# Moving each DMA transpose from behind a stored output to between the loads

## The chip, the cores and the metric

The kernel runs on one core of one Trainium2 chip. The metric is the device time of one execution in microseconds (us), where lower is better. Before the change the median of the first three executions was 312.18 us (311.15 to 312.39). Each comparison below names the number of executions. Now and then an execution is slower than the rest of the same kernel at a lower TensorE clock; the record calls one slow that is over 1.5% above the fastest.

## The reference

The reference is a retention layer (attention with a decay in place of softmax) followed by a two-layer block with the activation h·cos(h):

```python
# q, k, v: (8 batches, 8 heads, 576 positions, 64) float32
scores = (1 / sqrt(64)) * q @ k.transpose(0, 1, 3, 2)
ret    = scores * Dmat          # gamma[h] ** (i - j) for i >= j, else 0
attn   = ret @ v                # -> x: 4608 tokens x 512
h      = x @ w_in               # w_in: 512 x 2048
out    = (h * cos(h)) @ w_out   # w_out: 2048 x 512; out: 4608 x 512 float32
```

## The kernel before

The 4608 tokens are 36 groups of 128. Each group goes through these steps:

1. `load`: three DMAs (q, k, v; 256 KB each) bring the group in. SyncE (SP) issues them.
2. `prep`: GpSimd scales q and k by the decay and casts them to bf16 (tile `qks`), and casts v.
3. `transposes`: the matmuls of the scores read q and k with the head dimension on the partitions (tile `qkT`, 64 x 128 in the timelines below). For groups 0 to 7 TensorE does it; from group 8 on it is one DMA transpose from `qks` to `qkT`, which SP issues too.
4. `scores`, `state`, `attn_out`, `mm1`, `mm2`: the matmuls on TensorE. The order of TensorE's instructions is fixed by hand.
5. The output of the group is copied out of PSUM by ScalarE and stored by a DMA that SP issues as well.

So one queue, that of SP, issues loads, transposes and stores, one after the other in the order of the program (its timelines below show S7, T16, L19, S8, T17 before, and S7, L19, T17, S8 after). What is issued when is decided in `feed(s)`, which runs right behind the store of group `s`:

```python
def transposes(g, banks=None, only=(0, 1)):
    qks, vb, qkT, qT = tiles["a", g]
    if g >= N_PE_T:                                   # N_PE_T = 8
        nc.sync.dma_start(qkT, qks.rearrange("s m h d -> s (m h d)"), transpose=True)
        return
    ...  # cut: the same on TensorE, for groups below 8

def mm2(n, tsi, et, c0=0, c1=DM):
    ...  # cut: one output matmul; at the last one of a group:
        nc.scalar.copy(ot, ps)
        s = starts[n] // P + tsi
        nc.sync.dma_start(out[s * P : (s + 1) * P, c0:c1], ot)   # the store of group s
        feed(s)

def feed(s):
    nonlocal loaded, prepared, transposed
    while transposed < min(prepared, s + 10):
        transposes(transposed)
        transposed += 1
    while loaded < min(NG, 2 * s + 8, s + 13):
        load(loaded)
        loaded += 1
    while prepared < min(NG, loaded, 2 * s + 7, s + 11):
        prep(prepared)
        prepared += 1
        if transposed < N_PE_T:
            transposed += 1
```

The scores of two groups are issued together. The pair that matters here is 16 and 17, near the end of the stage of groups 8 to 11:

```python
def scores2(g):
    if g < NG:
        scores(g, "a")
        scores(g + 1, "b")
...  # cut
(52, lambda: (attn_out([g + 2, g + 3], "m"), scores2(g + 4))),   # g = 12 here
```

In this text S8 is the store of group 8, L19 the three loads of group 19, T17 the DMA transpose of group 17.

## Time and profile before

| | before |
|---|---|
| span of the profiled execution | 309.7 us |
| TensorE (PE) busy | 299.9 us, 97% |
| PE's longest wait after the start | 1.3 us, on the transpose T17 |
| T17 issued / landed | 113.53 / 118.17 us |
| groups whose scores follow their transpose's landing by under 1 us | 11, 15, 17 |

In the profiles, PE is TensorE, PEld its weight loads, DVE VectorE, ACT ScalarE, POOL GpSimd, SP SyncE; a q behind a name (SPq) means that engine's instruction queue, and PEclk is the clock that TensorE was granted. L173 is line 173 of the kernel; L173 makes the scores (`sc`), L287 the output matmuls (`o`). PSUM is where this kernel has the results of its matmuls.

From the page of the kernel before: the line of PE, the slices of the PE clock and of the DMA engines (each digit is a tenth, 40 slices), and the chain of work that ended last, by engine.

```profile
span 309.7 us, 5653 instructions
...
PE 299.9 (97%) x2328; PEld 171.5 (55%) x2361; DVE 176.1 (57%) x179; ACT 116.8 (38%) x136; POOL 97.4 (31%) x120
...
PEclk9999999999999999999999999999999999999999
DMA  8999999999999999999991899379935510110012
...
PE 89%; SPq 5%; DMA 4%; issue 1%; ACT 0%; DVE 0%; ACTq 0%
```

TensorE bounds the kernel (97% busy, 89% of the chain), so a change to DMA order can only be worth what PE waits for DMA. The second thing to see is the DMA row: for the first 20 slices, some 155 us, the DMA engines are at 8 or 9 tenths. In that stretch a transfer lands when its turn in the queue has come (e6 and e7 below test this: each load added ahead of L19 put its landing off by about 1.4 us).

From the wait view for PE, before: who PE waited for, in us in total, how often, and the longest.

```profile
engine line waited for: us in total, times, longest us
PE o L287 <- issue: 1.6, 10, 0.2
PE sc L173 <- DMA qkT<-qks: 1.3, 1, 1.3
```

The ten pieces of "issue" are missing records and not waits: 33 matmul records are absent here (2328, against 2361 in the profile after), and the line is gone in a profile that has them all. The 1.3 us is the one wait that the order of the transposes can reach. In the timeline of PE, before, it stands at 118 us (start, time taken, what, and in brackets the idle time before it):

```profile
116.51 0.40 PE L173 MATMUL sc<-qkT 64*128 64x128 bf16 x8
118.21 0.40 PE L173 MATMUL sc<-qkT 64*128 64x128 bf16 x8 [1.31 <-DMA qkT<-qks]
118.77 2.54 PE L287 MATMUL o<-w_out_sb,gT 128*128 128x512 bf16 x11 [0.16 <-issue]
```

The scores of group 16 run at 116.51, those of group 17 have to wait. In the row of the weight loads the gap before group 17 is 1.48 us:

```profile
118.21 0.23 PEld L173 LDWEIGHTS <-qkT 64*128 64x128 bf16 x8 [1.48 <-DMA qkT<-qks]
```

That measure is used from here on, because with it the accounts further below come out to 0.02 us.

Why T17 is late shows in the timeline of SP, before, around its issue:

```profile
107.34 1.17 SPq L298 DMA_DIRECT2D out_dram<-ot  x1
108.62 1.30 SPq L146 DMA_TRANSPOSE qkT<-qks  x1
109.97 0.70 SPq L107 DMA_DIRECT2D fq<-in_q_dram  x1
110.72 0.63 SPq L107 DMA_DIRECT2D fk<-in_k_dram  x1
111.39 0.97 SPq L107 DMA_DIRECT2D fv<-in_v_dram  x1
112.46 0.96 SPq L298 DMA_DIRECT2D out_dram<-ot  x1
113.53 1.33 SPq L146 DMA_TRANSPOSE qkT<-qks  x1
```

These are S7, T16, L19 (three rows), S8, T17. SP is never idle between them, and it is far behind: S7 is issued at 107.34 us, while ScalarE copied that output at 85.29 us. T17 comes behind S8 although its data were ready by 105 us.

### The profile page before, as it was taken

Reading aid. Unit: us, or ns where it says so; the run is one execution under the profiler, and the core shown is the slowest. Engines: PE = TensorE matmul, PEld = TensorE weight load, DVE = VectorE, ACT = ScalarE, POOL = GpSimd, SP = SyncE. Lnnn points to the kernel's source line nnn. Section 1 sums busy time; section 2 is a strip of 40 time slices with the busy share of each in tenths; the row PEclk is TensorE's granted clock in tenths of the full one; section 3 lists DMA queues with packets and bytes.
Section 4 is the critical chain, followed back from the end, with each engine's and each line's share of the span. In section 5 each row is a group of like instructions: output and inputs, shape, how many; then the busy total and the mean of one; then the engine's idle time right before and its main releaser. Section 6 shows DMA issues by size and latency. Waiting matters only on the chain.

```text
span 309.7 us, 5653 instructions
## 1 busy us (share of the span) xinstructions
PE 299.9 (97%) x2328; PEld 171.5 (55%) x2361; DVE 176.1 (57%) x179; ACT 116.8 (38%) x136; POOL 97.4 (31%) x120
## 2 busy tenths in 40 slices
PE   8899999999999998999999999999999999999996
PEld 3578547757588554445544554455445544554444
DVE  5766425555777764665567655755576556724610
ACT  2666234715045211650264116511551056015611
POOL 2740066644553564361533153305430000000000
PEclk9999999999999999999999999999999999999999
DMA  8999999999999999999991899379935510110012
GB/s 209 213 210 207 202 231 218 204 217 213 196 231 193 225 235 202 235 208 162 232 248 40 189 214 236 43 153 238 228 62 70 135 37 0 36 68 34 2 64 71
DMA packets 148697, 49.65 MB, mean 160 GB/s; under 512 B 138688, under 2 KB 144192, under 8 KB 148672
## 3 DMA queue, kind: packets, MB, share of 16 engines
q1 hardware_dynamic: 144448, 45.10, 75.3%
q0 software_dynamic: 4224, 4.19, 8.2%
q8 instruction: 18, 0.29, 0.4%
q14 instruction: 7, 0.06, 0.1%
HBM read 36.70 MB, written 9.44 MB: 149 GB/s over the span
## 4 chain that ended last, share of the span: by engine, by line
PE 89%; SPq 5%; DMA 4%; issue 1%; ACT 0%; DVE 0%; ACTq 0%
PE h L270 40%; PE o L287 38%; SPq L107 3%; PE ov L243 3%; PE sc L173 3%; DMA fv<-in_v_dram 2%; PE st L201 2%; PE ov L230 2%; DMA qkT<-qks 1%; PE tr L151 1%; SPq L146 0%; DVE xT L255 0%; SPq L298 0%; SPq L325 0%; ACT vb L158 0%
## 5 line engine op out<-in xcount | busy, mean ns | idle before, releaser
L287 PE MATMUL o<-w_out_sb,gT 128*128 128x512 bf16 (+2 forms) x583 | 131.1, 368 | 2.6 <-issue 1.6
L270 PE MATMUL h<-xT,w_in_sb 128*128 128x512 bf16 (+2 forms) x826 | 127.1, 313 | 0.5
L279 DVE TENSOR_TENSOR gT<-h,cosh 128x1024 bf16<-128x1024 f32 x72 | 88.2, 1225 | 57.5 <-ACT cosh L278 57.4
L270 PEld LDWEIGHTS <-w_in_sb 128*128 128x128 bf16 x832 | 75.9, 98 | 50.2 <-issue 0.4
L278 ACT ACTIVATE cosh<-h,half_pi 128x1024 f32<-128x1024 f32 x72 | 80.2, 1114 | 51.8 <-PE h L270 51.8
L287 PEld LDWEIGHTS <-gT 128*128 128x128 bf16 x608 | 55.2, 98 | 56.9 <-issue 0.6
L132 POOL TENSOR_TENSOR qks<-fq,gq 128x512 bf16<-128x512 f32 x32 | 33.4, 1043 | 109.7 <-DMA fq<-in_q_dram 109.7
L296 ACT COPY ot<-o 128x512 f32<-128x512 f32 (+2 forms) x38 | 21.4, 564 | 121.8 <-PE o L287 117.0
L133 POOL TENSOR_TENSOR qks<-fk,gk 128x512 bf16<-128x512 f32 x35 | 36.5, 1043 | 11.6 <-DMA fk<-in_k_dram 10.0
L182 DVE TENSOR_TENSOR ret<-sc,tri 128x1024 bf16<-128x1024 f32 x32 | 37.9, 1216 | 2.9 <-PE sc L173 2.9
L210 DVE TENSOR_TENSOR sb<-st,diag_105 128x512 bf16<-128x512 f32 x32 | 22.0, 686 | 27.8 <-PE st L201 27.8
L255 DVE CAST xT<-ov 128x1024 bf16<-128x1024 f32 (+1 forms) x17 | 19.7, 1161 | 25.8 <-PE ov L243 25.8
L139 POOL CAST vb<-fv 128x512 bf16<-128x512 f32 x32 | 19.6, 611 | 8.6 <-DMA fv<-in_v_dram 7.1
L201 PEld LDWEIGHTS <-qks 128*128 128x128 bf16 (+1 forms) x128 | 9.2, 97 | 7.5 <-issue 1.3
L201 PE MATMUL st<-vb,qks 128*128 128x128 bf16 (+1 forms) x128 | 12.4, 219 | 0.0
L173 PEld LDWEIGHTS <-qkT 64*128 64x128 bf16 x288 | 8.1, 94 | 7.3 <-ACT qkT L156 2.3
L243 PE MATMUL ov<-ret,vb 128*64 128x128 bf16 x288 | 12.1, 222 | 0.0
L173 PE MATMUL sc<-qkT 64*128 64x128 bf16 x256 | 10.4, 218 | 1.3 <-DMA qkT<-qks 1.3
L230 PEld LDWEIGHTS <-sb 128*128 128x128 bf16 x128 | 8.3, 98 | 4.3 <-issue 0.5
L243 PEld LDWEIGHTS <-vb 128*64 128x64 bf16 x288 | 8.6, 109 | 2.0
L156 ACT COPY qkT<-tr 128x512 bf16<-128x512 bf16 x12 | 6.6, 588 | 8.2 <-PE tr L151 8.2
L230 PE MATMUL ov<-qkT,sb 128*128 128x128 bf16 (+1 forms) x116 | 8.8, 215 | 0.0
(45 smaller groups left out, 54.3 us busy)
## 6 DMA issues: line engine op xcount, KB each, us to landing
out_dram<-ot SPq DMA_DIRECT2D x35, 256.0 KB, 4.1
fk<-in_k_dram SPq DMA_DIRECT2D x32, 256.0 KB, 4.9
fv<-in_v_dram SPq DMA_DIRECT2D x32, 256.0 KB, 5.1
fq<-in_q_dram SPq DMA_DIRECT2D x28, 256.0 KB, 4.3
w_in_sb<-in_moe_w_in_dram POOLq DMA_DIRECT2D x4, 512.0 KB, 8.9
w_out_sb<-in_moe_w_out_dram POOLq DMA_DIRECT2D x4, 512.0 KB, 16.1
fq_110<-in_q_dram SPq DMA_DIRECT2D x2, 512.0 KB, 4.4
fq<-in_q_dram SPq DMA_DIRECT2D x8, 128.0 KB, 4.2
```

The source lines that it names most:

```text
L132: nc.gpsimd.tensor_tensor(out=qks[:, 0], in0=fq, in1=tq, op=ALU.mult)
L133: (nc.vector if g == 3 else nc.gpsimd).tensor_tensor(out=qks[:, 1], in0=fk, in1=tk, op=ALU.mult)
L173: nc.tensor.matmul(ps[:, he, hg, :], lhsT=qkT[d0 : d0 + D, HG + hg, :], rhs=qT[d0 : d0 + D, hg, :], start=True, stop=True,)
L182: nc.vector.tensor_tensor(out=ret.rearrange("p a b i -> p (a b) i"), in0=ps.rearrange("p a b i -> p (a b) i"), in1=mask.unsqueeze(1).to_br ...
L201: nc.tensor.matmul(ps[:, hg, :], lhsT=qks[p0:, 1, 2 * hg : 2 * hg + 2, :].rearrange("s h d -> s (h d)"), rhs=vb[p0:, 2 * hg : 2 * hg + 2, ...
L210: nc.vector.tensor_tensor(out=sb, in0=ps, in1=diag2.unsqueeze(1).to_broadcast([P, HG, P]), op=ALU.mult,)
L230: nc.tensor.matmul(ps[:, x, hg, :n], lhsT=sb[:, hg, :], rhs=qT[:, hg, :n], start=(hg == 0), stop=False, skip_group_check=True,)
L243: nc.tensor.matmul(ps[he * D : he * D + D, x, hg, :], lhsT=vb[:, 2 * hg + he, :], rhs=ret[:, he, hg, :], start=(g % PER == 0 and hg == 0), ...
L270: nc.tensor.matmul(ps[:, j, :], lhsT=w_in_sb[:, dg, (et + j) * P : (et + j + 1) * P], rhs=xT[:, dg, c0 : c0 + w], start=(dg == 0), stop=(d ...
L278: nc.scalar.activation(cosh, ps, ACTF.Sin, bias=half_pi, scale=1.0)
L279: nc.vector.tensor_mul(gT[:, et : et + m, c0 : c0 + w], ps, cosh)
L287: nc.tensor.matmul(ps, lhsT=gT[:, et, tsi * P : (tsi + 1) * P], rhs=w_out_sb[:, et, c0:c1], start=(et == 0), stop=(et == ET - 1),)
```

## The change

Its intent: a transpose should not have to wait for the next stored output. It is issued in the same feed as its own group's `prep`, as soon as two more loads stand behind its group's loads, so that GpSimd has time to prepare it (1.04, 1.05 and 0.61 us for the three instructions of a group in the profile before, from 102.66 us on), and it alternates with loads in place of coming in twos.

```diff
     def feed(s):
         nonlocal loaded, prepared, transposed
-        while transposed < min(prepared, s + 10):
-            transposes(transposed)
-            transposed += 1
-        while loaded < min(NG, 2 * s + 8, s + 13):
-            load(loaded)
-            loaded += 1
-        while prepared < min(NG, loaded, 2 * s + 7, s + 11):
-            prep(prepared)
-            prepared += 1
-            if transposed < N_PE_T:
+        while True:
+            while prepared < min(loaded, NG, 2 * s + 7, s + 11):
+                prep(prepared)
+                prepared += 1
+                if transposed < N_PE_T:
+                    transposed += 1
+
+            if N_PE_T <= transposed < min(prepared, s + 11) and (
+                transposed <= loaded - 3 or loaded == NG
+            ):
+                transposes(transposed)
                 transposed += 1
+            elif loaded < min(NG, 2 * s + 8, s + 13):
+                load(loaded)
+                loaded += 1
+            else:
+                break
```

## The prediction

> What bounds the kernel now. TensorE. PE is busy (page) 299.9 of 309.7 us (97%), and has 89% of the chain of work that ended last. PE's idle gaps sum to about 7 us before its last matmul, and the wait view names the causes: 1.3 us at the start, 1.3 us once in the scores (L173) for a DMA transpose into qkT, 1.6 us "issue" in ten pieces. So the only PE idle time that this change can reach is the waits on transposes.
>
> Why that wait exists. In the timeline of SP, from 31 to 135 us the queue issues without a pause, each 256 KB load about 1.1 us after the one before; the DMA row shows 9 tenths. The queue is late: the store of token group 7 is issued at 107.3 us, though its copy ran on ScalarE at 85 us. So DMA throughput times everything here. From issue, landing and use in the trace, by group (landing to use): group 11 lands 84.49, used 84.53; 15: 107.92, used 108.36; 17: issued 113.53, lands 118.17, PE waits from 116.9 to 118.21. All others have 3.9 us or more.
>
> What changes. Nothing is added or removed, only the queue's order. Before: S2 T8 L10 L11, S3 T9 T10 L12 L13, S4 T11 T12 L14 L15, S5 T13 T14 L16 L17, S6 T15 L18, S7 T16 L19, S8 T17 (S store, T transpose, L load). After: S2 L10 T8 L11 T9, S3 L12 T10 L13 T11, S4 L14 T12 L15 T13, S5 L16 T14 L17 T15, S6 L18 T16, S7 L19 T17, S8. So every odd transpose up to 15, and every one from 16 on, comes one store earlier; 10, 12 and 14 come one load later, but they have 10 to 18 us of slack.
>
> Costs. (1) A store's turn in the queue is 1.0 to 1.1 us, so T11, T15, T17 go that much earlier. (2) A transpose holds SP for 1.3 us against 0.57 us for an unhindered load. After each of the pairs T9 T10, T11 T12, T13 T14 the next load lands 2.24, 1.91, 2.15 us after the transpose before it, where 1.2 is usual; after the single T8 it is 1.2. Estimate from these: the pairs drain the DMA queue for 0.7 to 1.0 us each, and alternating saves about 2.5 us of queue time before T17. Then T17 is issued near 110 to 111 us and lands near 115, before 116.9. The preparation on GpSimd is done in time (group 17: by 105 us). [...] in the trace no transpose before 120 us waited for its own group's preparation.
>
> On the critical path: 1.3 us at 118, and 0 to 1 us in executions where T11 or T15 fall late. Predicted 310.6 us, range 309.6 to 312.0; faster by over 2% 0.01, within 2% 0.98, slower 0.01.
>
> Right or wrong would show: the wait "sc L173 <- DMA qkT" gone or under 0.3 us; PE busy time unchanged; T11, T15, T17 landing 1 to 4 us before use; no double gap in landings at 74 to 99 us; store 8 issued no later than before; span near 308.3 us.
>
> Wrong if the DMA queue gains no time (then about 0.3 us of the wait remains), transposes slow the loads between them, or SP stalls on GpSimd.

## More of the kernel before

The weight loads also show a small wait on T11 at 84 us, which the list of PE hides:

```profile
84.10 0.23 PEld L173 LDWEIGHTS <-qkT 64*128 64x128 bf16 x8 [0.42 <-issue]
84.53 0.22 PEld L173 LDWEIGHTS <-qkT 64*128 64x128 bf16 x8 [0.20 <-DMA qkT<-qks]
```

## The result, and the profile after

| | before | after |
|---|---|---|
| median of 6 executions, same rounds | 311.88 us (311.09 to 312.68) | 309.90 us (309.86 to 310.39) |
| ratio of fast runs | | 0.994 (95%: 0.992 to 0.996) |
| span of the profiled execution | 309.7 us | 308.0 us |
| T17 issued / landed | 113.53 / 118.17 us | 111.83 / 116.07 us |
| wait on T11, on T17 (gap before the weight load) | 0.20, 1.48 us | 0, 0 us |

A ratio is the mean time of one kernel's fast runs over that of the other's of the same rounds, so not quite the ratio of the medians that stand beside it. In these rounds the gain is clear of the noise, though under 2%. On two other chips it was not clear: there the ratios are 0.999 (0.996 to 1.002) and 0.998 (0.996 to 1.001), see e8 and e10.

The same lines of the page, after:

```profile
span 308.0 us, 5686 instructions
...
PE 301.3 (98%) x2361; PEld 171.1 (56%) x2361; DVE 176.1 (57%) x179; ACT 116.8 (38%) x136; POOL 97.3 (32%) x120
...
PEclk9999999999999999999999999999999999999999
DMA  8999999999999999999990999299935310010012
...
PE 92%; SPq 3%; DMA 2%; DVE 1%; issue 1%; ACT 0%; ACTq 0%; DVEq 0%
```

PE's busy time seems to grow by 1.4 us, but no record is missing now: a second profile of the kernel before, which has all 2361 (e5), shows 302.0 us. The chain is now PE to 92%, and its share of DMA and SP has fallen: the piece that led from PE to T17 and on into the SP queue is no longer in it. In the wait view for PE, after, no line names `qkT<-qks` as a DMA any more; these are its first lines:

```profile
engine line waited for: us in total, times, longest us
PE idle L164 <- DVE zeros L351: 1.3, 1, 1.3
PE tr L392 <- DVE qs_111 L381: 0.8, 2, 0.4
PE tr L151 <- POOL qks L133: 0.6, 2, 0.4
```

These three belong to the first 20 us. The timeline of PE shows the scores of 16 and 17 in one piece of 16 matmuls, and the weight loads at 84 us the same for 10 and 11:

```profile
116.31 0.62 PE L173 MATMUL sc<-qkT 64*128 64x128 bf16 x16
116.86 2.76 PE L287 MATMUL o<-w_out_sb,gT 128*128 128x512 bf16 x12
```

```profile
84.10 0.45 PEld L173 LDWEIGHTS <-qkT 64*128 64x128 bf16 x16 [0.42 <-issue]
```

The timeline of SP, after: S7, L19, T17, S8. T17 now comes ahead of S8.

```profile
108.76 0.52 SPq L298 DMA_DIRECT2D out_dram<-ot  x1
109.34 0.42 SPq L107 DMA_DIRECT2D fq<-in_q_dram  x1
109.82 0.69 SPq L107 DMA_DIRECT2D fk<-in_k_dram  x1
110.55 1.17 SPq L107 DMA_DIRECT2D fv<-in_v_dram  x1
111.83 2.14 SPq L146 DMA_TRANSPOSE qkT<-qks  x1
114.06 0.53 SPq L298 DMA_DIRECT2D out_dram<-ot  x1
```

The 1.7 us between the two spans are as long as these two waits: 0.20 + 1.48 = 1.68 us. Whether they are the cause is tested in e4 and in the accounts.

### The profile page after: what moved, and what is told of

It reads as the page before. It is cut to its first block, busy times and chain, and to the rows that moved or that the text cites. A ratio compares the mean times of both kernels' runs of the same rounds, so it can differ in the third digit from the quotient of the medians.

```text
span 308.0 us, 5686 instructions
## 1 busy us (share of the span) xinstructions
PE 301.3 (98%) x2361; PEld 171.1 (56%) x2361; DVE 176.1 (57%) x179; ACT 116.8 (38%) x136; POOL 97.3 (32%) x120
## 4 chain that ended last, share of the span: by engine, by line
PE 92%; SPq 3%; DMA 2%; DVE 1%; issue 1%; ACT 0%; ACTq 0%; DVEq 0%
PE h L270 40%; PE o L287 40%; PE ov L243 3%; SPq L107 3%; PE sc L173 3%; DMA fv<-in_v_dram 2%; PE st L201 2%; PE ov L230 2%; PE tr L151 1%; DVE xT L255 0%; DVE ret L182 0%; SPq L331 0%; ACT vb L158 0%; ACT xT L255 0%; ACT ot L296 0%
## 5 line engine op out<-in xcount | busy, mean ns | idle before, releaser
L287 PE MATMUL o<-w_out_sb,gT 128*128 128x512 bf16 (+2 forms) x608 | 134.8, 368 | 0.3 <-DVE ret L182 0.3
```

What stands on the lines that cost most here:

```text
L287: nc.tensor.matmul(ps, lhsT=gT[:, et, tsi * P : (tsi + 1) * P], rhs=w_out_sb[:, et, c0:c1], start=(et == 0), stop=(et == ET - 1),)
```

## The experiments

Two theories of why T17 no longer comes late. Theory A: its place ahead of the store. Theory B: the alternation with loads, which keeps the DMA queue from draining. The prediction had put 1.0 to 1.1 us on A and about 2.5 us on B. All kernels gave the correct result. The first four ran on one chip, the next four on another, the last two on a third; "before" has its own figure for each. The changed kernel was not run on the first of these chips, so e1 to e4 can be compared with before, but only across chips with the whole change.

### e1: ahead of the store, but still in twos

```diff
-        while transposed < min(prepared, s + 10):   # at the head of feed
-            transposes(transposed)
-            transposed += 1
...
+        while N_PE_T <= transposed < min(prepared, s + 11) and (   # at its end
+            transposed <= loaded - 3 or loaded == NG
+        ):
+            transposes(transposed)
+            transposed += 1
```

> The same transposes in each feed as in the changed kernel (T17 ahead of store 8, T11 ahead of store 4, T15 ahead of store 6), but at the end of the feed behind all its loads, the pairs back to back as before. Theory A (the gain is the place ahead of the store): no wait of the scores for a transpose over 0.2 us, 309.9 to 310.4 us, 1.5 to 2.0 us under before. Theory B (the gain is the alternation, which keeps the DMA queue from draining): the pairs drain the queue again, T17 lands about 1 us later than in the changed kernel (117 us), a wait of about 0.5 us remains, 310.5 us or more.

Measured: 310.93 us median of 6 against 312.48 of 11 before, ratio 0.996 (0.993 to 0.999). In the profile T17 landed at 117.47 us, with a wait of 0.91 us; none on T11. Taken alone this speaks for B, but see the table of landings below.

### e2: alternating, but behind the store

```diff
-        while transposed < min(prepared, s + 10): ...
-        while loaded < min(NG, 2 * s + 8, s + 13): ...
+        due, upto = min(prepared, s + 10), min(NG, 2 * s + 8, s + 13)
+        while transposed < due or loaded < upto:
+            if transposed < due:
+                transposes(transposed)
+                transposed += 1
+            if loaded < upto:
+                load(loaded)
+                loaded += 1
```

> The pairs are broken up by loads, but every transpose stays behind the store that it stood behind before (T17 behind store 8). Theory A: most of the wait remains: T17 lands about 117.3 us (118.2 less at most 0.9 of queue time), wait 0.4 to 1.3 us, 310.7 to 311.8 us. Theory B: no wait, T17 lands before 116.5 us, 309.9 to 310.3 us.

Measured: 311.54 us median of 6, ratio 0.997 (0.994 to 0.999). T17 landed at 117.66 us; waits of 0.58 us on T11 and 0.46 us on T17. B's expectation (no wait, landing before 116.5) fails, and landing, wait and time are all as A expected. Taken alone this speaks for A.

### e3: one swap in the old order

```diff
             prep(prepared)
             prepared += 1
             ...
+        if s == 7:                      # T17 ahead of S8, nothing else
+            transposes(transposed)
+            transposed += 1
```

> One swap in the old order: T17 ahead of store 8 and nothing else. Theory A: the large wait at 118 us is gone or under 0.3 us, the 0.2 us of T11 at 84 us may stay: 310.0 to 310.6 us. Theory B (alternation): T17 gains only its store's turn of about 0.9 us and lands at 117.3 us, a wait of 0.4 us or more remains, 310.6 us or more.

Measured: 310.86 us median of 6, ratio 0.995 (0.992 to 0.998). The timeline of SP of this run shows T16, L19, T17, S8:

```profile
109.38 1.30 SPq L146 DMA_TRANSPOSE qkT<-qks  x1
...
112.11 0.91 SPq L107 DMA_DIRECT2D fv<-in_v_dram  x1
113.13 2.27 SPq L146 DMA_TRANSPOSE qkT<-qks  x1
115.50 0.52 SPq L298 DMA_DIRECT2D out_dram<-ot  x1
```

T17 landed at 117.63 us; waits of 0.62 us on T11, which this kernel does not touch, and 0.40 us on T17. Landing (117.3), wait (0.4 us or more) and time (310.6 us or more) are as B expected, the wait only just. So e1 and e3 speak for B and e2 for A: each half of the change alone left 0.4 to 0.9 us of wait. Waits of this size vary as much between executions of one kernel (e5 below), so the three runs do not decide.

### e4: the order of before, and the scores of 17 later

```diff
-(52, lambda: (attn_out([g + 2, g + 3], "m"), scores2(g + 4))),
+(52, lambda: (attn_out([g + 2, g + 3], "m"), scores(g + 4, "a") if n == 3 else scores2(g + 4))),
+(60, lambda: scores(g + 5, "b") if n == 3 else None),
```

> The DMA order is that of before; TensorE does the scores of group 17 eight output matmuls (1.7 us) later. Theory A and B both say that the one wait at 118 us is the whole loss: no wait or under 0.3 us there though T17 lands near 118 us as before, 310.1 to 310.8 us. If the gain of the change came from elsewhere (faster DMA, other waits), the time stays at 311.5 us or more.

Measured: 310.76 us median of 6, ratio 0.994 (0.992 to 0.997): the size of the gain of the change, with the DMA order untouched. T17 landed at 118.49 us, as late as before, and the weight load after it shows only the 0.42 us that stand ahead of other scores that follow output matmuls, too (those of groups 8, 10 and 12):

```profile
119.06 0.23 PEld L173 LDWEIGHTS <-qkT 64*128 64x128 bf16 x8 [0.42 <-issue]
```

So taking away the wait on T17 is worth a gain of that size, whoever takes it away. A wait of 0.57 us on T11 stayed.

### e5 and e8: both kernels again; e6 and e7: more loads ahead of T17

e5 is the kernel before and e8 the changed kernel, without edits. e6 and e7 put one and two more loads, whose data nobody uses, ahead of L19 and T17 in the changed kernel:

```diff
     def feed(s):
         nonlocal loaded, prepared, transposed
+        for x in range(1 if s == 7 else 0):     # e7: range(2 ...)
+            nc.sync.dma_start(fq4[:, :, x, :], k[0, :, :P, :].rearrange("h s d -> s h d"))
```

> The kernel before, unchanged, for a second profile and the size of its scatter. If the waits on T11 and T17 are the whole difference to the changed kernel, its span is 308.05 us plus those two waits, to about 0.2 us, whatever they are in this execution; T17 lands between 117.5 and 119.5 us.

> The changed kernel with one more 256 KB load (never used) behind store 7, ahead of load 19 and T17. If DMA throughput sets when T17 lands, it lands one load's turn (1.1 to 1.2 us) later, 117.2 us, and the slack of 0.47 us becomes a wait of about 0.7 us: span 308.7 us, time 310.6 us. If the queue has room, nothing changes: 309.9 us.

> The same with two more loads: T17 lands at 118.4 us, a wait of about 1.9 us, span 309.9 us, time 311.8 us. If the queue has room: 309.9 us.

> The changed kernel, unchanged, on the same chip as the three others: 309.9 us within 0.3, no wait of the scores on a transpose over 0.2 us, T17 landing at 115.5 to 116.7 us.

On this chip the kernel before has a median of 311.31 us (7 executions).

- e5: the three fast ones of 4 executions took 310.77, 311.02 and 311.51 us; the fourth, 316.75 us, was slow. In the profile T17 landed at 117.33 us, just outside the expected range, with a wait of 0.71 us and none on T11: the same kernel waited 1.68 us in one execution and 0.71 us in another. The span, 308.89 us, is 308.05 + 0.71 us within 0.2, as expected.
- e8: 310.81 us median of 4 (310.29 to 311.88), ratio 0.999 (0.996 to 1.002), so not shown to be faster than before on this chip. No wait on T11 or T17; T17 landed at 116.52 us. The time missed its range: see the accounts below.
- e6: 314.87, 314.72, 311.45 us and one slow execution (316.19); ratio 1.006 (0.999 to 1.012). The one at 311.45 us ran at full clock, the others at a mean clock of 0.995. T17 landed at 119.35 us; waits of 0.65 us on T11, which stands ahead of the added load, and 2.23 us on T17.
- e7: 315.06 us median of 4, ratio 1.014 (1.009 to 1.019). T17 landed at 119.26 us; a wait of 2.42 us.

From S7's landing to L19's it took 3.52 to 3.57 us in the three profiles of the changed kernel, 4.96 us in e6 and 6.27 us in e7. So each added load of 256 KB costs its full turn, about 1.4 us (estimated at 1.1 to 1.2), and the queue has no room. That theory holds. T17 itself landed 2.2 and 0.9 us later than expected, of which 1.8 and 0.6 us are a later landing of S7, ahead of the added loads. And the spans, 313.0 and 312.9 us, are 4.3 and 3.0 us over what was expected. The added wait explains only part of that; the timeline of PE and the clock row of e7 explain most of the rest:

```profile
116.66 0.40 PE L173 MATMUL sc<-qkT 64*128 64x128 bf16 x8
119.31 0.40 PE L173 MATMUL sc<-qkT 64*128 64x128 bf16 x8 [2.25 <-DMA qkT<-qks]
119.64 2.66 PE L287 MATMUL o<-w_out_sb,gT 128*128 128x512 bf16 x8
```

```profile
PEclk9999999999999997999999999999999999999999
```

There is a 7 in the clock row. The clock records give 0.5 for 3.41 us, from 119.82 us on in e6 and from 120.63 us on in e7, 0.42 and 1.32 us after the scores of 17 began. From the scores of 17 to those of 18 it takes 24.08 us in both, and 22.43 us in the profile of the changed kernel: 1.65 us lost beside the wait itself. (Some 0.4 us more stands after the last matmul in both and has no explanation here.) Half the clock for 3.41 us should cost 3.41 × 0.5 = 1.71 us, an estimate from the clock records of these two profiles, and the trace shows 1.65. The half clock came after 2.06 us (e6) and 2.25 us (e7) of idle PE; after the 1.31 us of the kernel before, the clock stayed full. What sets it off was not tested.

### Landings: what the swap gives, and what the alternation gives

The records of every profile allow the two theories to be read apart. In all of these orders the same transfers stand between S2 and L19 (the extra loads of e6 and e7 apart), so the time from S2's landing to L19's tells what the alternation gives. What comes from L19 to T17 tells what the swap gives. In us:

| kernel | order | S2 to L19 | L19 to T17 |
|---|---|---|---|
| before | in twos, behind | 54.26 | 2.05 |
| e5 (before) | in twos, behind | 53.78 | 1.62 |
| e4 (same DMA order) | in twos, behind | 54.83 | 1.66 |
| e2 | alternating, behind | 54.01 | 1.67 |
| e3 | in twos, T17 ahead of S8 | 54.52 | 0.79 |
| e1 | in twos, ahead | 54.16 | 0.84 |
| after | alternating, ahead | 53.22 | 0.84 |
| e8 (after) | alternating, ahead | 53.47 | 0.82 |
| e10 (after, below) | alternating, ahead | 54.53 | 0.82 |

The last column falls into two groups without overlap: 1.75 us on average behind the store (1.62 to 2.05), 0.82 us ahead of it (0.79 to 0.84). So the swap gives 0.93 us on average, and at least 0.78 us between any two of these profiles. In the third column the old order has a mean of 54.29 and the changed kernel 53.74, a difference of 0.55 us, and executions of one and the same order differ by 1.05 and 1.31 us. Taken over all nine profiles, the five in twos have a mean of 54.31 and the four alternating ones 53.81, 0.50 us less. So about half a microsecond is the best guess for the alternation, and with this scatter these runs do not show that it gives anything. The predicted 2.5 us are not there: even the two profiles furthest apart (54.83 and 53.22) differ by 1.61 us. It also tells why e1, e2 and e3 could not decide by their waits: the size of the wait in one execution is set by this scatter as much as by the order.

### Accounts: where the scatter comes from

For every profile that stays at full clock, the span can be put together from three numbers: the shift of the scores of group 8 (77.78 us in the changed kernel; it tells how long the start took), and the two waits. The last column is the span less that of the changed kernel, 308.04 us.

| profile | start | T11 | T17 | sum | span − 308.04 |
|---|---|---|---|---|---|
| before | 0.00 | 0.20 | 1.48 | 1.68 | 1.69 |
| e5 (before) | 0.14 | 0 | 0.71 | 0.85 | 0.85 |
| e1 | 0.07 | 0 | 0.91 | 0.98 | 0.98 |
| e2 | 0.13 | 0.58 | 0.46 | 1.17 | 1.18 |
| e3 | 0.12 | 0.62 | 0.40 | 1.14 | 1.15 |
| e8 (after) | 0.44 | 0 | 0 | 0.44 | 0.44 |
| e10 (after) | 1.58 | 0 | 0 | 1.58 | 1.60 |

(e4 is left out: its sum is 0.59 us and its span 0.82 us longer, a difference of 0.23 us; the author puts it down to the split pair of scores, which was not tested.) In these profiles there are two sources of scatter, and the change touches one of them. In e10 the start alone took 1.58 us longer: in that profile PE waits for `w_in` (0.69 us at 18.55 us) and for the first copy out of PSUM (1.19 us at 20.79 us), long before any DMA transpose. In the first profile of the changed kernel these waits are 0 and 0.37 us.

### e9 and e10: more slack, beside the changed kernel again

```diff
-                transposed <= loaded - 3 or loaded == NG
+                transposed <= loaded - (2 if s == 3 or s >= 6 else 3) or loaded == NG
```

> The changed kernel, but in feeds 3 and from 6 on a transpose is due one load behind its own group's, not two: T11 ahead of load 13, T16 ahead of load 18, T17 ahead of load 19. T17 lands one load's turn (about 3 us) earlier, at 113 to 114 us, T11 at 80 to 81 us, if SP does not stall on GpSimd. If the scatter of the changed kernel (309.9 to 311.9 us over 10 executions) is its thin slack on T11 and T17, this one shows no wait and less scatter: median 309.8 to 310.2 us, highest under 310.6. If the scatter has other causes (the start), it is as wide as the changed kernel's on the same chip.

> The changed kernel once more, on the same chip as the one with nearer transposes: 309.9 to 310.8 us, with some executions over 310.6 us if its slack of 0.3 to 0.5 us on T11 and T17 is sometimes used up.

Measured on one chip, where before has 311.70 us (11 executions): e9 310.26 us median of 6 (309.87 to 311.57), ratio 0.996 (0.994 to 0.998); e10 311.06 us of 6 (310.33 to 312.54), ratio 0.998 (0.996 to 1.001). The timeline of SP of e9 has T17 right behind S7:

```profile
108.05 1.03 SPq L298 DMA_DIRECT2D out_dram<-ot  x1
109.19 1.30 SPq L146 DMA_TRANSPOSE qkT<-qks  x1
```

T17 lands at 113.40 us, 3.1 us before its use (0.3 to 0.5 us in the three profiles of the changed kernel), T11 at 79.11 us, 5.2 us before. SP did not stall on GpSimd: the wait view of SP names it for some transposes, but in before, after and e9 the preparation of each of the groups 8 to 18 was finished at least 1.3 us before its transpose was issued, so that name only marks what GpSimd happened to finish then. The scatter did not shrink as expected: the highest of e9 is 311.57 us, where under 310.6 was expected. The median of e10 missed its range, too (311.06, expected up to 310.8). In the profile of e10 the extra time is the start's; the executions without a trace may have other causes. So e9 has six times the slack or more, and on this chip it is faster than before clear of the noise while e10 is not, but it is not shown to be faster than the changed kernel: both profiles that started alike (after and e9) have a span of 308.04 us.

## Why the prediction was right, and which terms of it were not

- **What bounds the kernel, and what can be gained.** Right. PE was the bound; all that could be gained was the waits on transposes. The two waits add up to 1.68 us, the spans differ by 1.69 us. Predicted 310.6 us, measured 309.9 us, inside the range. The range (309.6 to 312.0) also holds the 311.88 us of the kernel before, so that being inside it says little about the mechanism.
- **Term 1, the store's turn.** Nearly right: 1.0 to 1.1 us predicted, 0.93 us measured on average (0.78 us at least).
- **Term 2, the alternation.** Mis-sized. "The pairs drain the DMA queue for 0.7 to 1.0 us each, and alternating saves about 2.5 us": measured about 0.5 us, less than the scatter. The gaps were real. In all four profiles with pairs at the head of `feed` (before, e3, e4, e5) the load behind each of the three pairs landed 1.91 to 2.38 us after the transpose before it. In the first profile of the changed kernel no load up to L19 landed more than 1.63 us behind a transpose, and the double gaps behind pairs at 74 to 99 us are gone, as predicted (in e10 two loads landed later than that, 1.91 and 2.68 us). But the whole stretch from S2 to L19 is hardly shorter. Other steps grew: T8, for one, landed 2.42 us behind L10, where it had landed 1.08 us behind S2. What failed is the step from a gap that goes to time that the queue gains. Why the time comes back elsewhere stays open. One sign: in the changed kernel T8 to T15 held SP for 2.0 to 2.5 us each, against 1.3 us as a rule before, while a store behind one took 0.5 us as a rule, against 0.6 to 1.2 us before. As the preparation was done by then, that hold is not GpSimd's.
- **So the slack was overstated.** T17 was to be issued at 110 to 111 and to land near 115 us; it was issued at 111.83 and landed at 116.07 us, 0.47 us before its use. T11 had 0.62 us and only T15 (3.52 us) the predicted 1 to 4 us. That T17's landing moved by 2.1 us in these two profiles is partly luck. Counted from S2's landing it is 2.25 us, of which 1.21 us are the step from L19 to T17 and 1.04 us an earlier L19; the latter is as much as two executions of one kernel differ. By estimate the swap alone would have brought T17 to 118.17 − 0.93 = 117.24 us and left a wait of about 0.7 us. In e10, where L19 was not earlier, no wait shows because the start, and so the use of T17, came 1.58 us later.
- **Store 8 no later.** Wrong: it was issued at 114.06 us against 112.46, since it now stands behind T17. It cost nothing, as no wait of PE names it.
- **A little more in other executions (0 to 1 us).** Partly right. In the three profiles of the old order T11 waited 0.20, 0 and 0.57 us (before, e5, e4), and T15 never caused a wait. What varied most was the main term: the wait on T17 was 1.48 us in one profile of before and 0.71 in another. The gain in the medians was 2.0 us in the first comparison, 0.5 and 0.6 us in the two later ones, where the ratios do not exclude that there is none; the start of the changed kernel alone moved by up to 1.6 us between profiles. In e6 and e7, with waits of 2.23 and 2.42 us, the halved clock added 1.65 us. Two of the eleven executions of before in the first experiment ran at a mean clock of 0.995, at 314.08 and 313.66 us, and one of six in e10, at 312.54 us. They have no trace; that a long wait was their cause, as in the profile of e6 with the same mean clock, is not shown.

Left open: whether the alternation gives anything at all, how large the gain is on other chips, and why the start takes up to 1.6 us longer in some executions.

## What to carry to other kernels

Here one queue issued all loads, transposes and stores, the DMA engines were at 8 or 9 tenths, and the place of a transfer in that queue set its landing: ahead of S8, T17 landed 0.82 us behind L19 on average, behind S8 1.75 us, and each load added ahead of L19 put its landing off by about 1.4 us. In such a case put the transfer that the bottleneck engine waits for ahead of those that nobody waits for, such as the stores here. Measure the slack (landing to use) of every such transfer and not only the waits, because a slack below the scatter of the landings (1.05 and 1.31 us here) can be a wait in some other execution: T11 waited 0, 0.20 and 0.57 us in three profiles of the old order. Don't sum up the gaps that a change closes as its gain: time the whole stretch, before and after, in more than one profile of each. Here the double gaps behind the pairs closed, while T8's step grew from 1.08 to 2.42 us, and the stretch from S2 to L19 became shorter by about 0.5 us and not by 2.5.

## What else the profiles show

- In the full queue of the changed kernel's first profile T17 and S8 are 256 KB each: the transpose T17 landed 0.84 us behind the load before it, and S8 0.72 us behind the transpose, while an added 256 KB load with rows of 256 bytes took about 1.4 us (e6, e7). So there a transpose was dearer than a store and cheaper than such a load; these are steps between landings, not bandwidths.
- A transpose of this size held the issuing queue for 1.30 us as a rule in the kernel before, where an unhindered load took 0.57 us, and for 2.0 to 2.5 us for T8 to T15 in the changed kernel.
- The landing of one transfer in the full queue scattered between executions by 1.0 to 1.3 us after 54 us of transfers.
